# Transposing queries, keys and attention outputs by DMA instead of on TensorE from batch 2 on, with output stores issued from GpSimd's queue and loads one step earlier

## The chip, the cores and the metric

The kernel runs on one core of a Trainium2 chip. The metric is device time in microseconds (us). Engines: PE is TensorE (PEld its weight loads), DVE is VectorE, ACT is ScalarE, POOL is GpSimd, SP is SyncE. DMAs are issued from POOL's queue (software descriptors) and from SP's queue (hardware descriptors).

## The reference

Attention with a relative position bias for 8 batches of 8 heads, 576 positions, head size 64; its output is x, 4608 x 512, which goes through a bilinear feed-forward network (FFN) of width 1536:

```python
scores = q @ k.T / 8 + bias[bucket(i - j)]          # per batch and head, 576 x 576
attn_out = softmax(scores) @ v
x = attn_out.transpose(0, 2, 1, 3).reshape(4608, 512)
out = ((x @ w_a) * (x @ w_b)) @ w_out
```

## The kernel before

It works in steps. Step s computes scores and exponentials for head pair s (32 pairs, four to a batch) and the value products of pair s - 1. From step 4 on it mixes in "units" of the FFN, for a chunk of 512 tokens from an earlier batch: a group of four matmuls each, 36 units to a chunk, nine to a step (about 11.9 us). So a chunk lasts four steps. Its last twelve units are the four output tiles, three units each, and these fall mostly at the end of a step 4b - 1 and in step 4b. I call step 4b the boundary.

TensorE transposes queries, keys and attention outputs, since matmuls need the head dimension on the partitions:

```python
def transposes(ps, src, p, tag):
    b, hp = divmod(p, 4)
    for t in range(NM):                       # NM = 4
        x = (st[p][tag][:, t, :, :] if early(b) else
             src[b % 2][:, 512 * t + 128 * hp:512 * t + 128 * hp + 128])
        nc.tensor.transpose(ps[:, 128 * t:128 * t + 128], x, ident[:, :])
# t_q(p): four of these for queries, one for both tails, copies PSUM -> SBUF on DVE
# t_k(p): four for keys, copies on DVE
def t_x(p, eng=None):                         # attention outputs of pair p -> xn, the FFN's input
    ps = ps_tr.tile([128, 1024], BF16, tag="tr", name=f"trx{p}")
    for jq in range(5):
        nc.tensor.transpose(ps[:, 128 * jq:128 * jq + 128], XG[p % 2][:, jq, :, :], ident[:, :])
    copy(eng, xn_sb[hp][:, SM * b:SM * b + SM], ps[:, 0:SM])
    ...
```

An output tile is copied from PSUM by ACT into `ob`, which has two slots (`wrk` has `bufs=2`), and stored from SP's queue. The FFN's PSUM pool also has two buffers:

```python
ob = wrk.tile([128, DM], FP32, tag="ob", name=f"ob{c}_{tt}")
nc.scalar.activation(out=ob[:, :], in_=po[:, :], func=ACTF.Copy)
...
nc.sync.dma_start(out=out[r0:r0 + 128, :], in_=ob[:, :])
```

Loads go out from POOL, which runs its queue in order:

```python
b = s // 4 + 1
if s > 4 and s % 4 == 1 and b < B:
    load_q(b, 0, 8); load_k(b, 0, 8); load_tails(b); load_v(b, 0, 8); load_vt(b)
```

The softmax here doesn't subtract the row's maximum and nothing guards it: scores larger than these inputs give would overflow.

Of the kernel before, what the change touches and what calls it, by code (L numbers as in the profile page):

```python
# [13 lines left out]
def kernel(  # L14
# [11 lines left out]
    nc = tc.nc  # L26
    FP32 = mybir.dt.float32
    BF16 = mybir.dt.bfloat16
# [3 lines left out]
    B, H, S, Dh = 8, 8, 576, 64  # L32
    NB = 32
    NM = 4
    SM = 128 * NM
    ST = S - SM
# [4 lines left out]
    NDF = DF // 128  # L41
    NMC = DM // 128
    NP = B * H // 2
    scale = 1.0 / 8.0

    const = ctx.enter_context(tc.tile_pool(name="const", bufs=1))
    wpool = ctx.enter_context(tc.tile_pool(name="wpool", bufs=1))
# [41 lines left out]
    qn = [wpool.tile([128, H * NM * Dh], BF16, name=f"qn{i}") for i in range(2)]  # L89
    kn = [wpool.tile([128, H * NM * Dh], BF16, name=f"kn{i}") for i in range(2)]  # L90
    vn = [wpool.tile([128, H * NM * Dh], BF16, name=f"vn{i}") for i in range(2)]
    qkt = [wpool.tile([128, H, Dh], BF16, name=f"qkt{i}") for i in range(2)]
    vm = [wpool.tile([128, H, NM, Dh + 1], BF16, name=f"vm{i}") for i in range(2)]
    vt = [wpool.tile([128, H // 2, 2, Dh + 1], BF16, name=f"vt{i}") for i in range(2)]

    QT = [wpool.tile([128, S + 2 * ST], BF16, name=f"QT{i}") for i in range(3)]
    KT = [wpool.tile([128, SM + 2 * ST], BF16, name=f"KT{i}") for i in range(3)]
# [12 lines left out]
    def early(b):  # L110
        return b < 2
# [24 lines left out]
    def load_v(b, h0, h1):  # L136
        load4(v, vn[b % 2], b, h0, h1)

    def load_tails(b):
        for src, o in ((q, 0), (k, 64)):  # L140
            nc.gpsimd.dma_start(out=qkt[b % 2][o:o + 64, :, :],
                                in_=src[b, :, SM:S, :].transpose([1, 0, 2]))

    def load_vt(b):
        for hh in range(2):
            nc.gpsimd.dma_start(  # L146
                out=vt[b % 2][64 * hh:64 * hh + 64, :, hh, 0:Dh],
                in_=v[b, hh:H:2, SM:S, :].transpose([1, 0, 2]))
# [84 lines left out]
        nc.vector.memset(KT[i][64:128, SM:SM + ST], 0.0)  # L233


    st = [dict() for _ in range(NP)]

    def copy(eng, out, in_):
        if eng is nc.scalar:
# [23 lines left out]

    def t_q(p, eng=None):
        b, hp = divmod(p, 4)
        ps = ps_tr.tile([128, 1024], BF16, tag="tr", name=f"trq{p}")
        transposes(ps, qn, p, "qr")
        nc.tensor.transpose(ps[:, SM:SM + 128], qkt[b % 2][:, 2 * hp:2 * hp + 2, :], ident[:, :])  # L268
        qT, kT = QT[p % 3], KT[p % 3]
        if early(b):  # L270
            copy(eng, qT[:, 0:SM].rearrange("d (p t) -> d p t", t=NM),
                 ps[:, 0:SM].rearrange("d (t p) -> d p t", t=NM))
            copy(eng, qT[:, SM:S], ps[:, SM:S])
        else:
            copy(eng, qT[:, 0:S], ps[:, 0:S])
        for hh in range(2):
            r = slice(64 * hh, 64 * hh + 64)
            nc.vector.tensor_copy(out=kT[r, SM + ST * hh:SM + ST * hh + ST], in_=ps[r, S:S + ST])
            nc.vector.tensor_copy(out=qT[r, S + ST * hh:S + ST * hh + ST], in_=ps[r, SM:S])

    def t_k(p, eng=None, pool=None, tag="tr"):
        b, hp = divmod(p, 4)
        ps = (pool or ps_tr).tile([128, 1024], BF16, tag=tag, name=f"trk{p}")
        transposes(ps, kn, p, "kr")
        copy(eng, KT[p % 3][:, 0:SM], ps[:, 0:SM])
        st[p]["at"] = [None] * NM

    def v_in(b, h0, h1):
        if b < 2:
# [4 lines left out]


    def qk(p, t0):
        qT, kT = QT[p % 3], KT[p % 3]
        for t in (t0, t0 + 1):
            ps = ps_sc.tile([128, 2, 512], FP32, tag="sc", name=f"qk{p}_{t}")
            for hh in range(2):  # L300
                r = slice(64 * hh, 64 * hh + 64)
                nc.tensor.matmul(out=ps[:, hh, :], lhsT=kT[r, 128 * t:128 * t + 128],  # L302
                                 rhs=qT[r, 0:SM], start=True, stop=True)
            st[p]["ps", t] = ps

    def ex(p, t):
# [9 lines left out]


    def qk_tail(p):
        hp = p % 4
        qT, kT = QT[p % 3], KT[p % 3]  # L320
        ps = ps_sc.tile([128, 2, 512], FP32, tag="sc", name=f"qkt{p}")
        for t in range(NM):
            nc.tensor.matmul(
                out=ps[:, 0, :].rearrange("p (h t c) -> p h t c", h=2, t=NM)[:, :, t, :],
                lhsT=kT[:, 128 * t:128 * t + 128], rhs=qT[:, S:S + 2 * ST],
                start=True, stop=True)
        nc.tensor.matmul(out=ps[:, 1, :], lhsT=kT[:, SM:SM + 2 * ST], rhs=qT[:, 0:SM],
                         start=True, stop=True)
        pt = ps_tr.tile([128, 512], FP32, tag="tr", name=f"qktt{p}")
        nc.tensor.matmul(out=pt[:, 0:ST], lhsT=kT[:, SM:SM + 2 * ST], rhs=qT[:, SM:S],  # L330
                         start=True, stop=True)
        st[p]["ps"] = (ps, pt)

    def ex_tail(p):
# [55 lines left out]

    def t_x(p, eng=None):
        b, hp = divmod(p, 4)
        ps = ps_tr.tile([128, 1024], BF16, tag="tr", name=f"trx{p}")
        for jq in range(5):
            nc.tensor.transpose(ps[:, 128 * jq:128 * jq + 128], XG[p % 2][:, jq, :, :], ident[:, :])  # L395
        copy(eng, xn_sb[hp][:, SM * b:SM * b + SM], ps[:, 0:SM])
        copy(eng, xn_sb[hp][:, SM * B + ST * b:SM * B + ST * b + ST], ps[:, SM:S])
        st[p].clear()
# [22 lines left out]
    def ff_o(c, tt, part):  # L421
        if part == 0:
            ff["po"] = ps_ff.tile([128, 512], FP32, tag="ffn", name=f"po{c}_{tt}")
        po = ff["po"]
        for df in range(4 * part, 4 * part + 4):
            nc.tensor.matmul(out=po[:, :], lhsT=g_sb[df][:, 128 * tt:128 * tt + 128],  # L426
                             rhs=wo_sb[:, df, :], start=(df == 0), stop=(df == NDF - 1))
        if part == 2:
            ob = wrk.tile([128, DM], FP32, tag="ob", name=f"ob{c}_{tt}")
            nc.scalar.activation(out=ob[:, :], in_=po[:, :], func=ACTF.Copy)  # L430
            if c < B:
                r0 = S * c + 128 * tt
                nc.sync.dma_start(out=out[r0:r0 + 128, :], in_=ob[:, :])
            else:
                for hh in range(2):
                    r0 = S * (2 * tt + hh) + SM
                    nc.sync.dma_start(out=out[r0:r0 + ST, :], in_=ob[64 * hh:64 * hh + 64, :])

    units = []
    for c in range(NCH):  # L440
# [55 lines left out]
    for s in range(4, NP + 1):  # L496
        new = s < NP
        U = "unit"
        A = lambda *jq: (lambda: [av(s - 1, j) for j in jq])
        steps = []  # L500
        if new:
            steps += [lambda: (qk(s, 0), ex(s, 0))]
        if s == 4:
            steps += [A(0, 1, 2), lambda: ex(s, 1), lambda: t_q(s + 1), A(3, 4),
                      lambda: mul(s, 0), lambda: t_x(s - 1), U, lambda: mul(s, 1), U,
                      lambda: (qk(s, 2), ex(s, 2)), U, lambda: ex(s, 3), lambda: t_k(s + 1), U,
                      lambda: mul(s, 2), U, lambda: mul(s, 3), lambda: (qk_tail(s), ex_tail(s)),
                      U, U, lambda: mul_tail(s)]
        elif new:
            steps += [U, lambda: ex(s, 1), A(0, 1, 2), U, lambda: mul(s, 0)]  # L510
            if s + 1 < NP:
                steps += [lambda: t_q(s + 1)]
            steps += [U, lambda: mul(s, 1), lambda: (qk(s, 2), ex(s, 2)), U, lambda: ex(s, 3)]
            if s + 1 < NP:
                steps += [lambda: t_k(s + 1)]
            steps += [U, lambda: mul(s, 2), A(3, 4), U, lambda: mul(s, 3),
                      lambda: (qk_tail(s), ex_tail(s)), U, lambda: t_x(s - 1), U,
                      lambda: mul_tail(s), U]
        else:
            steps += [A(0, 1, 2), U, U, U, A(3, 4), U, U, U, lambda: t_x(s - 1), U, U, U]  # L520
        reorder(s + 1)
        b = s // 4 + 1
        if s > 4 and s % 4 == 1 and b < B:
            load_q(b, 0, 8)
            load_k(b, 0, 8)
            load_tails(b)
            load_v(b, 0, 8)
            load_vt(b)
        quota = quotas.get(s, 9)
        seen, put = 0, 0  # L530
        nu = sum(1 for x in steps if x is U)
        for x in steps:
            if x is U:
                seen += 1
                n = (quota * seen + nu - 1) // nu - put
                put_units(n)
                put += n
            else:
                x()
        if new:  # L540
            v_next(s)
# [31 lines left out]
```

## Time and profile before

| | before |
|---|---|
| time | 450.62 us (450.6 to 450.64, 2 runs) |
| PE busy | 424.7 us, 95% of the span |
| chain of waits that ended last | PE 83% |
| 85 to 350 us: PE busy, granted clock | 262.64 of 265 us, 1.00 |

The first lines are from the page: busy time and share of each engine; the chain by engine. The last is a line of the windows view: the stretch, its length, then busy us and instruction counts of PE, PEld, DVE, ACT and POOL, the granted clock, the DMA share and GB/s.

```profile
PE 424.7 (95%) x3578; PEld 221.1 (49%) x3643; DVE 287.4 (64%) x838; ACT 245.8 (55%) x350; POOL 88.9 (20%) x117
...
PE 83%; DVE 10%; DMA 3%; issue 2%; ACT 1%; SPq 0%; DVEq 0%; ACTq 0%
...
85.00:350.00 265.00, 262.64 (x2402) 140.53 (x2446) 188.22 (x547) 160.41 (x224) 43.29 (x54) 1.00 0.43 52
```

TensorE is the limit after the ragged start. What a transpose costs is read from the timeline (start, duration, engine, line, operation), at the starts of the matmuls around it: durations overlap, starts do not.

```profile
161.44 0.38 PE L406 MATMUL pa_6_2485<-xn_122,wa_114 128*128 128x512 bf16 x1
161.65 0.38 PE L406 MATMUL pa_6_2485<-xn_123,wa_114 128*128 128x512 bf16 x1
161.87 0.39 PE L262 MATMUL trk_2494<-ident,kn_96 128*128 128x128 bf16 x4
162.09 0.38 PE L416 MATMUL pb_6_2500<-xn_120,wb_117 128*128 128x512 bf16 x1
```

Two matmuls of a group are 0.215 us apart; with four transposes in between it is 0.44 us (161.65 to 162.09). So four cost 0.225 us, and five, read in the same way, 0.285 us.

The queues of SP and POOL at one boundary, from the timeline. The four stores of a chunk go out as soon as their tile is copied; four query loads (and four key loads) keep POOL busy 3.5 us.

```profile
180.48 0.33 SPq L433 DMA_DIRECT2D out_dram<-ob_0_2749  x1
184.94 0.33 SPq L433 DMA_DIRECT2D out_dram<-ob_1_2818  x1
189.08 0.33 SPq L433 DMA_DIRECT2D out_dram<-ob_2_2875  x1
192.42 0.33 SPq L433 DMA_DIRECT2D out_dram<-ob_3_2914  x1
...
207.26 3.53 POOL L123 DMA_DIRECT2D qn_93<-in_q_dram  x4 [18.47 <-PE trq_3162 L268]
210.76 3.54 POOL L132 DMA_DIRECT2D kn_95<-in_k_dram  x4
```

### The profile page before, as it was taken

The numbers are of one execution on the slowest core, as the hardware profiler recorded it, in microseconds if no ns is written. First come the engines' busy times: TensorE is split into PE (matmuls) and PEld (weight loads), VectorE is DVE, ScalarE is ACT, GpSimd is POOL, SyncE is SP. The second block draws the span as 40 slices with busy tenths as digits, with TensorE's granted clock in tenths as the row PEclk, the third lists the DMA queues.
The fourth block names the chain that finished last, engine by engine and source line by source line (L and its number), as shares of the span: only waits on it lengthen the run. The fifth ranks groups of instructions, "written<-read, shape, count | busy, mean of one in ns | idle before, by whom it ended". The sixth has DMA issues, their size and how long they took to land.

```text
span 449.3 us, 9012 instructions
## 1 busy us (share of the span) xinstructions
PE 424.7 (95%) x3578; PEld 221.1 (49%) x3643; DVE 287.4 (64%) x838; ACT 245.8 (55%) x350; POOL 88.9 (20%) x117
## 2 busy tenths in 40 slices
PE   5676999999999999999999999999999999999995
PEld 2264455555555555555555555555555554444442
DVE  5579789668766787577856786587658862330320
ACT  2678566556655665566556665566556652322321
POOL 9456365010801070105200350100000000000000
PEclk8579999999999999999999999999999999999999
DMA  9999999420942097207912290200010002002004
GB/s 101 219 200 203 192 148 76 82 65 1 107 72 63 15 84 72 77 25 49 104 49 54 16 137 27 76 1 1 23 71 2 1 1 94 1 0 93 1 1 94
DMA packets 87370, 30.35 MB, mean 68 GB/s; under 512 B 64760, under 2 KB 82712, under 8 KB 87328
## 3 DMA queue, kind: packets, MB, share of 16 engines
q0 software_dynamic: 80144, 18.88, 45.0%
q1 hardware_dynamic: 6992, 10.86, 7.3%
q8 instruction: 28, 0.46, 0.4%
q14 instruction: 14, 0.11, 0.1%
q10 hardware_dynamic: 192, 0.03, 0.0%
HBM read 39.18 MB, written 9.45 MB: 108 GB/s over the span
## 4 chain that ended last, share of the span: by engine, by line
PE 83%; DVE 10%; DMA 3%; issue 2%; ACT 1%; SPq 0%; DVEq 0%; ACTq 0%
DMA Wt<-bias_tab 2%; DVE XG_111 L387 1%; DVE g_125 L419 1%; DVE g_124 L419 1%; PE warm L208 1%; PE po_1_1335 L426 1%; PE po_0_1275 L426 1%; DMA bias_tab<-tab_sb 1%; PE po_1_2057 L426 1%; PE po_1_4869 L426 1%; PE po_1_3463 L426 1%; PE po_1_2760 L426 1%; PE po_1_4166 L426 1%; PE po_2_1403 L426 1%; PE po_3_6071 L426 1%
## 5 line engine op out<-in xcount | busy, mean ns | idle before, releaser
L416 PEld LDWEIGHTS <-wb_118 128*128 128x128 bf16 x144 | 12.4, 97 | 16.6 <-issue 5.6
L406 PEld LDWEIGHTS <-wa_114 128*128 128x128 bf16 x144 | 12.5, 98 | 15.3 <-issue 3.4
L416 PEld LDWEIGHTS <-wb_117 128*128 128x128 bf16 x144 | 12.4, 97 | 14.9 <-issue 4.7
L406 PEld LDWEIGHTS <-wa_113 128*128 128x128 bf16 x144 | 12.5, 98 | 14.6 <-issue 3.0
L416 PEld LDWEIGHTS <-wb_116 128*128 128x128 bf16 x144 | 12.3, 97 | 14.9 <-issue 5.1
L406 PEld LDWEIGHTS <-wa_115 128*128 128x128 bf16 x144 | 12.7, 98 | 13.4 <-issue 2.5
L123 POOL DMA_DIRECT2D qn_93<-in_q_dram x12 | 11.0, 925 | 38.6 <-PE trq_3162 L268 18.5
L123 POOL DMA_DIRECT2D qn_94<-in_q_dram x12 | 10.6, 886 | 40.2 <-PE trq_2459 L268 18.5
L146 POOL DMA_DIRECT2D vt_104<-in_v_dram x8 | 4.9, 620 | 53.7 <-PE av_3_2848 L376 17.3
L132 POOL DMA_DIRECT2D kn_95<-in_k_dram x12 | 10.6, 906 | 6.8 <-DVE qr_844 L251 6.6
L146 POOL DMA_DIRECT2D vt_103<-in_v_dram x8 | 5.0, 640 | 34.8 <-PE av_3_2145 L376 17.3
L132 POOL DMA_DIRECT2D kn_96<-in_k_dram x12 | 10.6, 912 | 0.0
L395 PEld LDWEIGHTS <-XG_112 128*128 128x128 bf16 x80 | 5.8, 98 | 5.4 <-DVE XG_112 L387 1.5
L395 PEld LDWEIGHTS <-XG_111 128*128 128x128 bf16 x80 | 5.8, 98 | 5.1 <-DVE XG_111 L387 1.8
L302 PEld LDWEIGHTS <-KT_108 64*128 64x128 bf16 x88 | 2.8, 95 | 10.7 <-issue 8.6
L419 DVE TENSOR_TENSOR g_124<-pb_0_5871,ha_0_5869 128x512 bf16<-128x512 f32 x1 | 0.7, 692 | 11.4 <-PE pb_0_5871 L416 11.4
L302 PEld LDWEIGHTS <-KT_109 64*128 64x128 bf16 x88 | 2.6, 95 | 10.4 <-issue 10.4
L426 PEld LDWEIGHTS <-g_124 128*128 128x128 bf16 x36 | 3.5, 97 | 7.0 <-issue 4.7
L302 PEld LDWEIGHTS <-KT_110 64*128 64x128 bf16 x80 | 2.4, 95 | 8.2 <-issue 8.1
L114 POOL DMA_DIRECT2D vn_98<-in_v_dram x5 | 4.2, 836 | 7.4 <-DVE vm_102 L291 6.8
L426 PEld LDWEIGHTS <-g_126 128*128 128x128 bf16 x36 | 3.5, 98 | 4.3
L426 PEld LDWEIGHTS <-g_134 128*128 128x128 bf16 x36 | 3.5, 98 | 4.3
(3194 smaller groups left out, 1643.6 us busy)
## 6 DMA issues: line engine op xcount, KB each, us to landing
qn_93<-in_q_dram POOLq DMA_DIRECT2D x16, 128.0 KB, 4.2
kn_95<-in_k_dram POOLq DMA_DIRECT2D x16, 128.0 KB, 5.1
qn_94<-in_q_dram POOLq DMA_DIRECT2D x16, 128.0 KB, 5.4
kn_96<-in_k_dram POOLq DMA_DIRECT2D x16, 128.0 KB, 4.9
wo<-in_moe_w_out_dram POOLq DMA_DIRECT2D x1, 1536.0 KB, 16.4
vn_97<-in_v_dram POOLq DMA_DIRECT2D x3, 512.0 KB, 7.1
vn_98<-in_v_dram POOLq DMA_DIRECT2D x3, 512.0 KB, 5.8
vn_97<-in_v_dram POOLq DMA_DIRECT2D x2, 256.0 KB, 10.7
```

Source lines behind the costliest of these rows:

```text
L114: nc.gpsimd.dma_start(out=dst[:, 256 * h0:256 * h1].rearrange("p (h x) -> p h x", x=256), in_=src[b, h0:h1, 0:SM, :].rearrange("h (p t) d ...
L123: nc.gpsimd.dma_start(out=qn[b % 2][:, :].rearrange("p (t h d) -> p t h d", h=H, t=NM)[:, t, h0:h1, :], in_=q[b, h0:h1, 128 * t:128 * t + ...
L132: nc.gpsimd.dma_start(out=kn[b % 2][:, :].rearrange("p (t h d) -> p t h d", h=H, t=NM)[:, t, h0:h1, :], in_=k[b, h0:h1, t:SM:NM, :].transp ...
L146: nc.gpsimd.dma_start(out=vt[b % 2][64 * hh:64 * hh + 64, :, hh, 0:Dh], in_=v[b, hh:H:2, SM:S, :].transpose([1, 0, 2]))
L208: nc.tensor.matmul(out=warm[:, :], lhsT=zero_sb[:, 0:128], rhs=zero_sb[:, :], start=True, stop=True)
L302: nc.tensor.matmul(out=ps[:, hh, :], lhsT=kT[r, 128 * t:128 * t + 128], rhs=qT[r, 0:SM], start=True, stop=True)
L387: nc.vector.tensor_tensor(out=xg[0:np_, j0:j0 + n, :, :], in0=pav[0:np_, s0:s0 + n, :, 0:Dh], in1=rc.unsqueeze(3).to_broadcast([np_, n, 2, ...
L395: nc.tensor.transpose(ps[:, 128 * jq:128 * jq + 128], XG[p % 2][:, jq, :, :], ident[:, :])
L406: nc.tensor.matmul(out=pa[:, :], lhsT=wa_sb[df // 4][:, mc, 128 * (df % 4):128 * (df % 4) + 128], rhs=xn_sb[mc][:, 512 * c:512 * c + 512], ...
L416: nc.tensor.matmul(out=pb[:, :], lhsT=wb_sb[df // 4][:, mc, 128 * (df % 4):128 * (df % 4) + 128], rhs=xn_sb[mc][:, 512 * c:512 * c + 512], ...
L419: nc.vector.tensor_tensor(out=g_sb[df][:, :], in0=pb[:, :], in1=ff["ha"][:, :], op=MULT)
L426: nc.tensor.matmul(out=po[:, :], lhsT=g_sb[df][:, 128 * tt:128 * tt + 128], rhs=wo_sb[:, df, :], start=(df == 0), stop=(df == NDF - 1))
```

## The change

Its intent is to take transposes off TensorE. From batch 2 on, four transposing DMAs a batch, issued from SP, turn queries, keys and their zero-padded tails; two a pair turn the attention outputs. Stores move from SP's queue to POOL's, so that SP's is free for transposes. The loads move one step earlier, to the boundary step, so that the transposes can follow in time.

```diff
+    def turn(b):
+        i = b % 2
+        for src, dst in ((qn, QTb), (kn, KTb)):
+            nc.sync.dma_start_transpose(
+                out=dst[i][:, :, :, :].rearrange("d t h p -> d (t h) p"), in_=src[i][:, :])
+        for src, dst in ((qtl, QTt), (ktl, KTt)):
+            nc.sync.dma_start_transpose(
+                out=dst[i][:, :, :], in_=src[i][:, :, :, :].rearrange("p h a d -> p (h a d)"))
 ... (t_q and t_k return at once for these batches; qk and qk_tail read QTb, KTb, QTt, KTt)
-        nc.tensor.matmul(out=pt[:, 0:ST], lhsT=kT[:, SM:SM + 2 * ST], rhs=qT[:, SM:S],
-                         start=True, stop=True)
+        for hh in range(2):
+            nc.tensor.matmul(out=pt[:, 0:ST], lhsT=kTt_(p), rhs=qTt_(p)[:, ST * hh:ST * hh + ST],
+                             start=(hh == 0), stop=(hh == 1))
 ... (t_x)
+        if p >= XD:                                        # XD = 8
+            nc.sync.dma_start_transpose(
+                out=xn_sb[hp][:, SM * b:SM * b + SM].rearrange("d (t p) -> d t p", t=NM),
+                in_=XG[p % 2][:, 0:4, :, :].rearrange("p j a d -> p (j a d)"))
+            ... (and the 64 tail rows)
+            return
 ... (ff_o)
-                nc.sync.dma_start(out=out[r0:r0 + 128, :], in_=ob[:, :])
+                nc.gpsimd.dma_start(out=out[r0:r0 + 128, :], in_=ob[:, :])
 ... (main loop)
-        if s > 4 and s % 4 == 1 and b < B:
+        if s % 4 == 0 and b < B and new:
             load_q(b, 0, 8)
             load_k(b, 0, 8)
             load_tails(b)
             load_v(b, 0, 8)
+        if s % 4 == 1 and b < B:
             load_vt(b)
+        if s % 4 == 3 and b < B:
+            turn(b)
```

More of the change, by code (lines that the diff above doesn't have):

```diff
@@ L43 @@
     NP = B * H // 2
+    XD = 8
     scale = 1.0 / 8.0
@@ L92 @@
     qkt = [wpool.tile([128, H, Dh], BF16, name=f"qkt{i}") for i in range(2)]
+    qtl = [wpool.tile([128, H // 2, 2, Dh], BF16, name=f"qtl{i}") for i in range(2)]
+    ktl = [wpool.tile([128, H // 2, 2, Dh], BF16, name=f"ktl{i}") for i in range(2)]
+    QTb = [wpool.tile([128, NM, H // 2, 128], BF16, name=f"QTb{i}") for i in range(2)]
+    KTb = [wpool.tile([128, NM, H // 2, 128], BF16, name=f"KTb{i}") for i in range(2)]
+    QTt = [wpool.tile([128, H // 2, 128], BF16, name=f"QTt{i}") for i in range(2)]
+    KTt = [wpool.tile([128, H // 2, 128], BF16, name=f"KTt{i}") for i in range(2)]
     vm = [wpool.tile([128, H, NM, Dh + 1], BF16, name=f"vm{i}") for i in range(2)]
@@ L139, in load_tails @@
     def load_tails(b):
+        if not early(b):
+            for src, dst in ((q, qtl), (k, ktl)):
+                for hh in range(2):
+                    nc.gpsimd.dma_start(
+                        out=dst[b % 2][64 * hh:64 * hh + 64, :, hh, :],
+                        in_=src[b, hh:H:2, SM:S, :].transpose([1, 0, 2]))
+            return
         for src, o in ((q, 0), (k, 64)):
@@ L233, with kT_, qT_, kTt_ @@
         nc.vector.memset(KT[i][64:128, SM:SM + ST], 0.0)
+    for i in range(2):
+        for x in (qtl, ktl):
+            nc.gpsimd.memset(x[i][0:64, :, 1, :], 0.0)
+            nc.gpsimd.memset(x[i][64:128, :, 0, :], 0.0)
     st = [dict() for _ in range(NP)]
+    def turn(b):
[6 more added lines that the diff above has]
+                out=dst[i][:, :, :], in_=src[i][:, :, :, :].rearrange("p h a d -> p (h a d)"))
+    def kT_(p, t):
+        b, hp = divmod(p, 4)
+        return KT[p % 3][:, 128 * t:128 * t + 128] if early(b) else KTb[b % 2][:, t, hp, :]
+    def qT_(p):
+        b, hp = divmod(p, 4)
+        return QT[p % 3][:, 0:SM].rearrange("d (t p) -> d t p", t=NM) if early(b) else QTb[b % 2][:, :, hp, :]
+    def kTt_(p):
+        b, hp = divmod(p, 4)
+        return KT[p % 3][:, SM:SM + 2 * ST] if early(b) else KTt[b % 2][:, hp, :]
+    def qTt_(p):
+        b, hp = divmod(p, 4)
+        return QT[p % 3][:, S:S + 2 * ST] if early(b) else QTt[b % 2][:, hp, :]
     def copy(eng, out, in_):
@@ L265, in t_q @@
         b, hp = divmod(p, 4)
+        if not early(b):
+            return
         ps = ps_tr.tile([128, 1024], BF16, tag="tr", name=f"trq{p}")
@@ L282, in t_k @@
         b, hp = divmod(p, 4)
+        st[p]["at"] = [None] * NM
+        if not early(b):
+            return
         ps = (pool or ps_tr).tile([128, 1024], BF16, tag=tag, name=f"trk{p}")
@@ L285, in t_k @@
         copy(eng, KT[p % 3][:, 0:SM], ps[:, 0:SM])
-        st[p]["at"] = [None] * NM
     def v_in(b, h0, h1):
@@ L296, in qk @@
     def qk(p, t0):
-        qT, kT = QT[p % 3], KT[p % 3]
+        qT = qT_(p)
         for t in (t0, t0 + 1):
@@ L301, in qk @@
                 r = slice(64 * hh, 64 * hh + 64)
-                nc.tensor.matmul(out=ps[:, hh, :], lhsT=kT[r, 128 * t:128 * t + 128],
-                                 rhs=qT[r, 0:SM], start=True, stop=True)
+                nc.tensor.matmul(out=ps[:, hh, :], lhsT=kT_(p, t)[r, :],
+                                 rhs=qT[r, :, :], start=True, stop=True)
             st[p]["ps", t] = ps
@@ L318, in qk_tail @@
     def qk_tail(p):
-        hp = p % 4
-        qT, kT = QT[p % 3], KT[p % 3]
         ps = ps_sc.tile([128, 2, 512], FP32, tag="sc", name=f"qkt{p}")
@@ L324, in qk_tail @@
                 out=ps[:, 0, :].rearrange("p (h t c) -> p h t c", h=2, t=NM)[:, :, t, :],
-                lhsT=kT[:, 128 * t:128 * t + 128], rhs=qT[:, S:S + 2 * ST],
+                lhsT=kT_(p, t), rhs=qTt_(p),
                 start=True, stop=True)
-        nc.tensor.matmul(out=ps[:, 1, :], lhsT=kT[:, SM:SM + 2 * ST], rhs=qT[:, 0:SM],
+        nc.tensor.matmul(out=ps[:, 1, :], lhsT=kTt_(p), rhs=qT_(p),
                          start=True, stop=True)
         pt = ps_tr.tile([128, 512], FP32, tag="tr", name=f"qktt{p}")
-        nc.tensor.matmul(out=pt[:, 0:ST], lhsT=kT[:, SM:SM + 2 * ST], rhs=qT[:, SM:S],
-                         start=True, stop=True)
+        for hh in range(2):
+            nc.tensor.matmul(out=pt[:, 0:ST], lhsT=kTt_(p), rhs=qTt_(p)[:, ST * hh:ST * hh + ST],
+                             start=(hh == 0), stop=(hh == 1))
         st[p]["ps"] = (ps, pt)
@@ L392, in t_x @@
         b, hp = divmod(p, 4)
+        if p >= XD:
+            nc.sync.dma_start_transpose(
+                out=xn_sb[hp][:, SM * b:SM * b + SM].rearrange("d (t p) -> d t p", t=NM),
+                in_=XG[p % 2][:, 0:4, :, :].rearrange("p j a d -> p (j a d)"))
+            o = SM * B + ST * b
+            nc.sync.dma_start_transpose(
+                out=xn_sb[hp][:, o:o + ST].unsqueeze(1),
+                in_=XG[p % 2][0:64, 4, :, :].rearrange("p a d -> p (a d)"))
+            st[p].clear()
+            return
         ps = ps_tr.tile([128, 1024], BF16, tag="tr", name=f"trx{p}")
@@ L436, in ff_o @@
                     r0 = S * (2 * tt + hh) + SM
-                    nc.sync.dma_start(out=out[r0:r0 + ST, :], in_=ob[64 * hh:64 * hh + 64, :])
+                    nc.gpsimd.dma_start(out=out[r0:r0 + ST, :], in_=ob[64 * hh:64 * hh + 64, :])
     units = []
```

## The prediction

> What bounds the kernel now. The windows view has TensorE busy 29.74 of every 30 us from 100 to 340 us, at granted clock 1.00, and the chain of waits is 83% PE. DVE (64%), ACT (55%) and POOL (20%) have room. After about 60 us time moves one for one with work taken from TensorE's stream, or a wait put into it.
>
> Removed. From pair 8 on, each pair loses 5 transposes for queries and their tail, 4 for keys and 5 for attention outputs. In the timeline, 4 key transposes push the next matmul group from the usual 0.215 us to 0.44 us after its predecessor (0.225 us net), a group of 5 to 0.50 us (0.285 us net). Per pair 0.285+0.225+0.285 = 0.795 us; 24 pairs: 19.1 us, all on the critical path. DVE's copies go too, worth nothing here. Added on TensorE: one 64-column matmul in each of 32 tails, estimated 0.04 us each, 1.3 us. Net about -18 us, 433 us, if everything else hides.
>
> What I expect not to hide:
> 1. Stores move behind loads. POOL's queue now has, in order, the first store of a chunk, the 13 loads of a batch, then stores two to four. In the trace four q loads take 3.53 us of POOL, four k loads 3.53, a 64-partition load 0.62, the v load 0.89: 10.5 us of issue. Today stores two to four follow the first by 4.4, 8.6 and 11.9 us, on SP's queue, and land in 2.0 us. Store two will be issued about 11.5 us after the first and lie behind the v load (5.8 to 7.1 us to landing), so it lands after 15 to 17.5 us. The output buffer has two slots: the fourth copy on ACT, due at about 11 us, waits for that store, 3 to 6 us. TensorE has about 1.8 us of work (scores and one FFN group) before it needs the same PSUM buffer. Estimate 1 to 4.5 us lost at each of 5 boundaries (steps 8, 12, 16, 20, 24): about 3 us each, 15 us. If TensorE idles long enough the clock can fall as well (the Trainium skill, "TensorE: Matmul & The Clock Gate", gives about 3.4 us of idle; this trace shows clock 0.50 only in its ragged start).
> 2. The last pair of a batch now reaches the FFN through a DMA. Today the PE transposes precede the chunk that reads them by about 3.5 us; a DMA takes 2 us or more to land. 0 to 1 us at each of 7 boundaries.
> 3. The last stores go by software descriptors: up to +1 us.
> The batch transposes (1.25 MB per batch) have a whole step, 11 us; the Trainium skill, "DMA: Bandwidth & Descriptors", latency table, gives 261 GB/s for transposing DMAs, an estimate of 5 us. No run here shows it yet. They should hide.
>
> Sum: 450.6 - 18 + 15 + 2 + 1, about 450. I predict 449 us, range 433 to 466; faster 0.28, same 0.45, slower 0.27.
>
> What would show it. Right: about 336 fewer transposes; steps of about 11.1 us where no batch load starts; gaps on TensorE and ACT at the start of the steps after 8, 12, 16, 20, 24, released by an output store; store two landing 15 us after store one. Wrong: if ACT never waits for store two, the time is near 434 us. If the batch transposes take over 11 us, TensorE waits for them at steps 8, 12, ... and the time goes beyond 466 us; likewise, at the first FFN group of each chunk, if a transposing DMA is much slower beside loads.

## The result, and the profile after

The changed kernel is correct and slower: 475.2 us (473.42 and 476.98, 2 runs) against 450.62. The ratio is 1.0551, 95% interval 1.0455 to 1.0646. A ratio here is the mean time of one kernel's fast runs over that of the other's of the same rounds, so it is not quite the ratio of the medians quoted.

The same lines of the changed kernel:

```profile
PE 420.8 (89%) x3280; PEld 206.3 (44%) x3339; DVE 248.8 (53%) x646; ACT 245.3 (52%) x350; POOL 119.9 (25%) x177
...
issue 41%; PE 32%; DMA 14%; POOL 11%; DVE 0%; ACT 0%; POOLq 0%; ACTq 0%; DVEq 0%
...
85.00:350.00 265.00, 236.95 (x1928) 115.60 (x1960) 139.42 (x336) 145.05 (x203) 68.27 (x94) 0.94 0.78 90
```

The trace has 298 matmuls fewer (336 transposes go and 32 tail matmuls come; a few records are missing). Yet PE's busy time fell by only 3.9 us, with a granted clock of 0.94 on average from 85 to 350 us; the same instructions with the clock at 1.00 there (e3 below) are busy for 409.4 us, 15.3 less than before. And in that stretch PE is now idle 28 us instead of 2.4. The chain of waits is no longer mostly PE's.

The view of waits (who waited for what; us in total, times, longest) names the places, for PE and then for ACT:

```profile
PE pb L473 <- ACT ob L487: 19.0, 5, 4.8
PE pa L463 <- DMA xn<-XG: 6.8, 4, 2.2
...
ACT ob L487 <- DMA out_dram<-ob: 43.1, 5, 9.6
```

Five times ACT waits some 8.6 us to copy an output tile, until an earlier store has freed its slot. Five times PE waits for that copy. Four times it waits for attention outputs that a DMA transposes. The numbers add up: 19.0 + 6.8 = 25.8 us, and PE's idle time rose by 28.05 - 2.36 = 25.7.

One boundary in the timeline, first the queue of POOL, then the last output transpose on SP's queue, then PE and ACT:

```profile
135.52 0.57 POOL L490 DMA_DIRECT2D out_dram<-ob  x1 [31.91 <-ACT ob L487]
136.08 3.54 POOL L130 DMA_DIRECT2D qn<-in_q_dram  x4
139.56 3.55 POOL L139 DMA_DIRECT2D kn<-in_k_dram  x4
143.02 1.34 POOL L150 DMA_DIRECT2D qtl<-in_q_dram  x2
144.24 1.34 POOL L150 DMA_DIRECT2D ktl<-in_k_dram  x2
145.45 1.03 POOL L121 DMA_DIRECT2D vn<-in_v_dram  x1
146.33 1.27 POOL L490 DMA_DIRECT2D out_dram<-ob  x2
153.99 0.55 POOL L490 DMA_DIRECT2D out_dram<-ob  x1 [6.38 <-ACT ob L487]
...
142.33 1.20 SPq L441 DMA_TRANSPOSE xn<-XG  x1
...
142.97 2.75 PE L483 MATMUL po<-wo,g 128*128 128x512 bf16 x11
149.03 0.38 PE L463 MATMUL pa<-xn,wa 128*128 128x512 bf16 x1 [2.01 <-DMA xn<-XG]
153.10 0.60 ACT L487 ACTIVATE ob<-po 128x512 f32<-128x512 f32 x1 [8.74 <-DMA out_dram<-ob]
153.75 1.86 PE L473 MATMUL pb<-xn,wb 128*128 128x512 bf16 x4 [2.96 <-ACT ob L487]
```

Read it from the top. Store one leaves at 135.5. Thirteen loads follow, 10.2 us of POOL's time. The copy of store two's tile had begun at 138.8 us, but the store leaves only at 146.3, behind all of them. The fourth tile is complete in PSUM at 145.7 (142.97 + 2.75). ACT copies it at 153.1, when store two's slot is free: 7.4 us late. Meanwhile the output transpose issued at 142.33 is there only at 149.03, 6.7 us later, where an undisturbed one takes 2.4 us. PE has two gaps, 2.0 us for that transpose and 3.0 us for the copy.

After the first gap the granted clock falls. This is the windows view, in four stretches of a quarter of a us; the clock is the third number from the end.

```profile
148.75:149.00 0.25, 0.00 (x0) 0.00 (x0) 0.00 (x0) 0.00 (x0) 0.00 (x0) 1.00 1.20 113
149.50:149.75 0.25, 0.25 (x11) 0.25 (x8) 0.00 (x0) 0.00 (x0) 0.00 (x0) 0.76 1.29 168
149.75:150.00 0.25, 0.25 (x9) 0.25 (x7) 0.00 (x0) 0.00 (x0) 0.00 (x0) 0.50 1.46 193
...
156.50:156.75 0.25, 0.25 (x2) 0.00 (x0) 0.25 (x1) 0.00 (x0) 0.00 (x0) 1.00 1.28 81
```

It is 0.50 from about 149.6 until about 156.4 (the stretches left out in between have 0.50 as well, up to the last one). So three things cost time at a boundary: the copy's wait, the late transpose, and a clock that is at half speed when work resumes.

### The profile page after: what moved, and what is told of

Its sections match the earlier page's. It is cut to its first block, busy times and chain, and to the rows that moved or that the text cites. A ratio compares the mean times of both kernels' runs of the same rounds, so it can differ in the third digit from the quotient of the medians.

```text
span 471.6 us, 8441 instructions
## 1 busy us (share of the span) xinstructions
PE 420.8 (89%) x3280; PEld 206.3 (44%) x3339; DVE 248.8 (53%) x646; ACT 245.3 (52%) x350; POOL 119.9 (25%) x177
## 4 chain that ended last, share of the span: by engine, by line
issue 41%; PE 32%; DMA 14%; POOL 11%; DVE 0%; ACT 0%; POOLq 0%; ACTq 0%; DVEq 0%
PE pb L473 10%; PE po L483 9%; PE pa L463 9%; DMA kn<-in_k_dram 4%; POOL qn L130 3%; DMA qn<-in_q_dram 3%; POOL kn L139 2%; DMA wa<-in_moe_w_a_dram 2%; DMA wb<-in_moe_w_b_dram 2%; PE av L423 2%; DMA vn<-in_v_dram 2%; PE qk L350 2%; DMA out_dram<-ob 1%; POOL out_dram L490 1%; POOL vt L160 1%
## 5 line engine op out<-in xcount | busy, mean ns | idle before, releaser
L357 ACT ACTIVATE at<-qk 128x1024 bf16<-128x1024 f32 x128 | 126.4, 1025 | 17.8 <-PE qk L350 17.8
L476 DVE TENSOR_TENSOR g<-pb,ha 128x512 bf16<-128x512 f32 x108 | 74.6, 691 | 111.3 <-PE pb L473 93.7
L473 PE MATMUL pb<-xn,wb 128*128 128x512 bf16 x410 | 113.2, 391 | 20.9 <-ACT ob L487 19.0
L463 PE MATMUL pa<-xn,wa 128*128 128x512 bf16 x421 | 114.7, 390 | 7.3 <-DMA xn<-XG 6.8
L467 ACT ACTIVATE ha<-pa 128x512 f32<-128x512 f32 x108 | 64.6, 598 | 76.5 <-PE pa L463 73.9
L483 PE MATMUL po<-wo,g 128*128 128x512 bf16 x410 | 99.4, 379 | 1.2
L362 DVE TENSOR_TENSOR at<-at,W 128x1024 bf16<-128x1024 bf16 x128 | 85.1, 683 | 9.3 <-ACT at L357 7.5
L463 PEld LDWEIGHTS <-wa 128*128 128x128 bf16 x432 | 39.9, 100 | 53.2 <-issue 16.2
L423 PE MATMUL av<-vm,at 128*128 128x65 bf16 x1024 | 49.9, 199 | 0.2 <-DVE at L362 0.2
L423 PEld LDWEIGHTS <-at 128*128 128x128 bf16 x1024 | 45.1, 101 | 6.6 <-DVE at L362 0.3
L414 PEld LDWEIGHTS <-att 128*128 128x128 bf16 x160 | 16.0, 100 | 17.1 <-issue 10.4
```

The lines of the kernel that those rows point to most:

```text
L357: nc.scalar.activation(out=at[:, :, :], in_=ps[:, :, :], func=ACTF.Exp, scale=scale)
L362: nc.vector.tensor_tensor(out=at[:, :, :], in0=at[:, :, :], in1=w[:, :, S - 1 + t:S - 1 + t - SM:-1], op=MULT)
L414: nc.tensor.matmul(out=pav[:, slot, :, :], lhsT=x, rhs=vt[i][:, hp, :, :], start=True, stop=True)
L423: nc.tensor.matmul(out=pav[:, slot, hh, :], lhsT=x, rhs=vm[i][:, 2 * hp + hh, t, :], start=False, stop=True, skip_group_check=True)
L463: nc.tensor.matmul(out=pa[:, :], lhsT=wa_sb[df // 4][:, mc, 128 * (df % 4):128 * (df % 4) + 128], rhs=xn_sb[mc][:, 512 * c:512 * c + 512], ...
L467: nc.scalar.activation(out=ha[:, :], in_=pa[:, :], func=ACTF.Copy)
```

## The experiments

Two theories stood at the start. Theory Q: the order of POOL's queue holds store two behind the loads, and the two output slots hand the delay to ACT and PE. Theory T: the transposing DMAs share the DMA engines with everything else and slow it, whichever queue the stores use. The kernel before took 450.2 to 450.9 us (medians). All results were correct.

| run | time, us | ratio to before | PE idle, 85 to 350 us | PE's wait for output copy | for attention outputs | for keys | clock, 85 to 350 us |
|---|---|---|---|---|---|---|---|
| changed kernel | 475.2 | 1.0551 | 28.1 | 19.0 | 6.8 | 0 | 0.94 |
| e1 stores on SP | 467.8 | 1.0378 | 23.7 | 0 | 9.0 | 13.2 | 0.96 |
| e2 four slots | 445.9 | 0.9905 | 9.9 | 0 | 7.7 | 0 | 0.99 |
| e3 loads later | 435.9 | 0.9682 | 2.2 | 0 | 0 | 0 | 1.00 |
| e4 outputs by PE | 490.9 | 1.0899 | 41.0 | 38.5 | 0 | 0 | 0.93 |
| e5 before, with the new queue order | 487.4 | 1.0847 | 25.1 | 22.3 | 0 | 0 | 0.96 |
| e7 gaps filled | 468.8 | 1.0397 | 9.4 | 3.5 | 1.2 | 0 | 1.00 |
| e10 stores on SP, loads held | 435.5 | 0.9662 | 2.2 | 0 | 0.4 | 0 | 1.00 |
| e12 v load later | 452.2 | 1.0043 | 14.0 | 3.0 | 7.1 | 0 | 1.00 |
| e11 loads later, outputs by PE | 441.5 | 0.9811 | 2.9 | 0 | 0 | 0 | 1.00 |
| e9 loads later, last stores on SP | 433.2 | 0.9618 | 2.2 | 0 | 0 | 0 | 1.00 |

The waits are of the whole span, and 85 to 350 us covers a different share of each kernel's work; both only serve to show what is there. A zero means that the view of waits lists none. One of e12's four runs (458.15 us) is slow; its time and ratio are from the other three (mean 452.28 us over 450.34). e8, a single run, is told in its section.

### e1: stores back on SP's queue

```diff
-                nc.gpsimd.dma_start(out=out[r0:r0 + 128, :], in_=ob[:, :])
+                nc.sync.dma_start(out=out[r0:r0 + 128, :], in_=ob[:, :])
```
(and the same for the last chunk)

> The changed kernel with one thing undone: output stores go out from SyncE's queue again; loads, DMA transposes all as in the change. Theory Q (POOL's queue holds store two behind 13 loads, two output slots make ACT and then TensorE wait): the 43 us of ACT waiting for an output store go to nearly 0, the 19 us of TensorE waiting for the output copy go to nearly 0, the four-step period of the disturbed chunks falls from about 52.7 us to about 46 to 47, and the time to 443 to 450 us. What stays is TensorE's wait for the last pair's transposed output beside the loads, about 2 us at each of 5 boundaries. Rival T (the transposing DMAs slow everything that shares the DMA engines, whichever queue the stores use): a store from SyncE still lands late, since it follows transposes and shares engines with loads, ACT still waits, and the time stays above 465 us.

Measured: 467.77 us. ACT no longer waits for a store at all, as theory Q has it, and stores land in 2.2 us (median). But the time lies in the range of rival T, above 465, though for another reason than the late store that T had named: a new wait took the place of the old one. Lines of the timeline, SP and POOL, and the wait on PE that ends them:

```profile
117.69 1.70 SPq L260 DMA_TRANSPOSE QTb<-qn  x1
119.37 0.90 POOL L121 DMA_DIRECT2D vn<-in_v_dram  x1 [16.59 <-DVE vm L339]
119.57 8.38 SPq L260 DMA_TRANSPOSE KTb<-kn  x1
...
133.06 0.60 PE L350 MATMUL qk<-QTb,KTb 64*128 64x512 bf16 x4 [3.99 <-DMA KTb<-kn]
```

With no store in POOL's queue, nothing holds the loads to the pace of the chunks. They run as far ahead as their buffers allow. The loads of later batches go out early, and the v load waits for its buffer and leaves exactly beside the batch's transposes. The transpose of keys is then issued over 8.4 us (3.6 us in the changed kernel) and takes 12.2 us to land instead of 5.7 (medians). So my expectation of 443 to 450 missed. Theory Q was right about the stores and silent about a second thing that the stores did in POOL's queue: they paced the loads. Theory T's mechanism, slowing beside loads, showed itself, though not on the stores.

### e2: four output slots

```diff
+    obp = ctx.enter_context(tc.tile_pool(name="obp", bufs=4))
-            ob = wrk.tile([128, DM], FP32, tag="ob", name=f"ob{c}_{tt}")
+            ob = obp.tile([128, DM], FP32, tag="ob", name=f"ob{c}_{tt}")
```

> The changed kernel with four output slots in place of two; stores still behind the loads on POOL's queue. Theory Q: store two still lands some 17 us after store one, but nobody waits for it within the chunk, so the ACT and TensorE waits vanish and the time is 443 to 450 us, as with the stores on SyncE. Rival T: the slots change little, above 465 us.

Measured: 445.91 us, in the range. Store two is still late, the waits for the slot are gone, and the late attention outputs are all that stays of PE's idle time: 9.86 - 2.16 = 7.7 us more than e3, and 7.7 us is that wait. This run shows that the two slots are the link between a late store and a stalled PE.

### e3: loads one step later, behind the chunk's stores

```diff
-        if s % 4 == 0 and b < B and new:
+        if s > 4 and s % 4 == 1 and b < B:
```

> The changed kernel with the batch's loads issued one step later (where the kernel before has them), after the chunk's four stores and after the last pair's transpose; stores still on POOL's queue. Theory Q with its second part (the last pair's transpose takes 6.7 us instead of 2.4 only because it runs beside the loads): both waits vanish, clock stays at 1.00 after 60 us, four-step period about 44.5 us throughout, time 431 to 437 us. Rival T: transposes beside loads still cost somewhere, time over 445 us. If the batch transposes now come too late for their step, TensorE waits for them at steps 8, 12, ... and the time is over 440.

Measured: 435.93 us, in the range; 0.9682 of the kernel before. The windows line and the chain of this run:

```profile
85.00:350.00 265.00, 262.84 (x2250) 131.30 (x2291) 163.67 (x396) 169.53 (x237) 71.05 (x98) 1.00 0.82 95
...
PE 87%; DVE 2%; issue 1%; ACT 0%; POOL 0%; POOLq 0%; DVEq 0%; ACTq 0%
```

One line of the program takes 39 us off the changed kernel (whose two runs lie 3.6 us apart, so the 39 is good to a few us). The loads now follow store four in POOL's queue and run when no output transpose is urgent: an output transpose beside them takes up to 7.7 us to land here too, but nobody waits for it. From store one to store one is 44.8 us (129.40, 174.22, 219.03 us), where the kernel before has 47.52 and the changed kernel 52.7 on average (135.52 to 346.30 us, four chunks). So the transposes on TensorE were worth 2.7 us a chunk, and the boundary costs 7.9 us.

### e4: attention outputs on PE again, the rest as changed

```diff
-    XD = 8
+    XD = NP
```

> The changed kernel with attention outputs transposed on TensorE again for all pairs; queries and keys still by DMA, stores still behind the loads. It adds 24 x 0.285 = 6.8 us of TensorE work. Theory Q: the end of each disturbed boundary is set by the landing of store two, 17.5 us after store one, so only the wait for the transposed output goes and the wait for the output copy grows by as much; time 470 to 481 us. Rival X (the late transposed output is what costs most): time 455 to 465 us.

Measured: 490.87 us, slower than either range. Removing the late output transposes gained nothing, but this run alone does not settle rival X, since it moved other transposes as well (below). e2 does: there the late outputs stay, PE waits 7.7 us for them, and the time is only 10 us above e3. Theory Q's number was too low here. The output transposes had been standing in SP's queue in front of the batch's, and so held them back. Without them the batch's transposes start as soon as the loads land, in the middle of the boundary:

```profile
147.83 3.85 SPq L260 DMA_TRANSPOSE QTb<-qn  x1
152.68 6.47 SPq L260 DMA_TRANSPOSE KTb<-kn  x1
```

There they meet the v load and store two (issued at 151.05). ACT's wait for a store grew from 43.1 to 54.9 us in total. The latest store took 10.4 us to land; in the changed kernel it was 7.6.

### e5: the kernel before, with only the new order of POOL's queue

```diff
-                nc.sync.dma_start(out=out[r0:r0 + 128, :], in_=ob[:, :])
+                nc.gpsimd.dma_start(out=out[r0:r0 + 128, :], in_=ob[:, :])
-        if s > 4 and s % 4 == 1 and b < B:
+        if s % 4 == 0 and b < B and new:
```
(`load_vt` stays at `s % 4 == 1`; the last chunk's stores move too)

> The kernel before, with only the change's queue order: stores issued from POOL, the batch's loads one step earlier, the late v tails where they were. No DMA transposes at all. Theory Q: store two again leaves POOL behind 12 loads, about 11 us after store one, lands behind the v load at about 16 us, and ACT's fourth copy, due at 11.9 us, waits some 4 us; TensorE loses 1 to 3 us at each of 5 boundaries; time 455 to 465 us. Rival T (only the transposes make the stores late): the time stays at 449 to 453 us.

Measured: 487.38 us. The waits of PE and ACT:

```profile
PE pb L416 <- ACT ob L430: 22.3, 5, 5.4
...
ACT ob L430 <- DMA out_dram<-ob: 38.6, 5, 8.8
```

There is no DMA transpose in this kernel (and 11 loads in front of store two, not the 12 that I had counted), and it loses 36.5 us (487.38 - 450.91). So theory T is not needed for the late stores; the queue order is enough. My number was too low here as in the prediction: ACT's wait was 38.6 us in five, 7.7 each, not 4, and I had again left out the clock (0.96).

### e7: the gaps filled with useless matmuls

```diff
+            late = s in (9, 13, 17, 21, 25)
+            steps += [lambda: fill(9)] if late else []     # 9 matmuls of zeros, 128x512
             steps += [U, lambda: ex(s, 1), A(0, 1, 2)]
+            steps += [lambda: fill(13)] if late else []
```

> The changed kernel with idle time of TensorE filled: at steps 9, 13, 17, 21, 25, 9 matmuls of zeros after the first scores and 13 after the first output products, 4.7 us of work at full clock in gaps of about 5 us. It adds work and takes no wait away. If the fall of the granted clock after the gaps is part of the loss: clock stays near 1.00 in these stretches and the time falls by 4 to 9 us, to 466 to 471. If it is not: 475 us or more.

Measured: 468.78 us, in the range: about 7 us faster by adding work ((1.0551 - 1.0397) x 450.6; the two intervals leave some 2 to 12 us). The windows line and ACT's wait:

```profile
85.00:350.00 265.00, 255.61 (x2082) 126.16 (x2123) 142.59 (x347) 148.09 (x208) 70.70 (x97) 1.00 0.79 92
...
ACT ob L487 <- DMA out_dram<-ob: 43.9, 5, 9.3
```

The clock stays at 1.00, and ACT's wait for stores is unchanged. So the fall of the clock is a cost of its own, about 7 of the 39 us, net of whatever the added matmuls cost.

### e8: stores on SP and the loads one step later in the program (one run)

The edits of e1 and e3 together.

> Stores from SyncE and the loads one step later in the program. POOL's queue then holds exactly the instructions of the run with stores on SyncE and loads early, in the same order. Theory R (with no store in POOL's queue nothing holds the loads back: they run steps ahead and meet the batch's transposes): as that run, 463 to 470 us, TensorE again waits for transposed keys. Rival (the place of the loads in the program decides): as the run with loads later and stores on POOL, 432 to 440 us.

Measured: 467.01 us in one run, as e1 and unlike e3; PE waits 12.5 us for keys. POOL's instructions are the same as in e1 and in the same order, and that decides. The place of the loads among the other engines' instructions in the program made less than 1 us of difference.

### e10: as e8, but the loads are held back

```diff
+            if "ob" in ff:       # the chunk's last output tile
+                nc.gpsimd.tensor_copy(out=gate_sb[0:1, 0:1], in_=ff["ob"][0:1, 0:1])
             load_q(b, 0, 8)
```
(and `ff["ob"] = ob` where the tile is copied)

> As the run before in this list, with one addition: before each batch's loads POOL copies one element of the chunk's last output tile, so the loads can't run ahead of the chunk's end. Stores stay on SyncE. Theory R: the loads no longer meet the transposes, the waits for transposed keys and outputs go, and the time is 431 to 438 us. Rival (stores and transposes in one queue of SyncE disturb each other): stays over 445 us.

Measured: 435.49 us. One element copied by POOL before each batch's loads takes 31.5 us off (467.01, a single run, minus 435.49). The rival, that stores and transposes in one queue of SP disturb each other, falls: they do not, to within what these runs resolve. Here it hardly matters which queue carries the stores (435.93 us in e3); when the loads run does.

### e12: only the v load later

```diff
             load_tails(b)
-            load_v(b, 0, 8)
         if s % 4 == 1 and b < B:
+            load_v(b, 0, 8)
             load_vt(b)
```

> The changed kernel with only the v load taken out from in front of the stores, to the next step; the 12 loads of queries, keys and tails stay in front. It splits the delay of store two: time to leave POOL's queue (about 10.6 us after store one instead of 11.4) and time behind the v load's data. If the v load's data is most of the lateness: store two lands 13.5 to 15 us after store one, ACT's wait falls from 8.6 to 2 to 4 us a boundary, TensorE's wait for the output copy to 0 to 1 us, and the transposed output of the last pair is still slow; time 444 to 455 us. If the order in POOL's queue alone is what counts: 468 to 474 us.

Measured: 452.15 us, the median of the three fast runs, in the range. At the boundary I looked at, store one left at 131.16, store two at 141.09, and the fourth copy began at 145.67: 14.5 us after store one, where it was 17.6 (153.10 - 135.52). ACT still waited 5.7 us, more than I expected, but PE's wait for the copy fell from 19.0 to 3.0 us. So of the 39 us, 23 (475.2 - 452.15) hung on the last, largest load in front of the stores; PE rode out most of the rest of ACT's wait.

### e11 and e9: what is left

e11 has the edits of e3 and e4; e9 has that of e3, and stores of the last two chunks from SP.

> Loads one step later, stores on POOL, and the attention outputs transposed on TensorE. It repeats the test of the transposed outputs where no load is in their way: 24 groups of five transposes at 0.285 us, so 6 to 7.5 us slower than the same kernel with outputs by DMA (435.9 us), 442 to 444 us. If the outputs by DMA cost TensorE hidden waits even there, the difference is smaller, under 4 us.

> Loads one step later, and the stores of the last two chunks, after the last loads and transposes, on SyncE's queue. Only the end differs: the last store is issued in two parts of about 0.5 us on POOL. If its way through POOL costs anything it is the last 1 us: 434 to 436 us.

Measured: 441.48 us for e11, 5.6 us slower than e3, just under the range of 442 to 444. So the attention outputs by DMA are worth nearly the 6.8 us of their transposes, once loads are out of their way. e9 ran in 433.17 us, just under its range of 434 to 436 and the best of all: 0.9618 of the kernel before, interval 0.9589 to 0.9646. In the profiles, the time from the end of the last output copy to the end is 3.9 us in e9 and 5.7 us in e3. That explains 1.8 us of the difference; the rest, 1 us, I leave open.

## Why the prediction was wrong

1. **What bounds the kernel, and the saving.** "After about 60 us time moves one for one with work taken from TensorE's stream": right. e3, with nothing in the way, has chunks 2.7 us shorter; the prediction's terms give 4 x (0.795 - 0.04) = 3.0 us. Over the whole run e3 saves 14.5 us and e9 17.0, of the 18 forecast.
2. **Step 1, the mechanism.** "POOL's queue now has, in order, the first store of a chunk, the 13 loads of a batch, then stores two to four": right in every link. e5 shows it without the transposes, e2 shows that the slots pass it on, e3 shows it gone.
3. **The size of a boundary: the step that failed.** The sum priced a boundary at "about 3 us each, 15 us" for the copy's wait and about 2 us in all for the last pair's outputs: 17 us, nearly all at five boundaries. A boundary costs 7.9 us, five cost 39. The copy's wait itself was not far off: PE waited 19.0 us for it, 2.4 to 4.8 us at a boundary, against "1 to 4.5". ACT's wait, "3 to 6" us, was 7.4 us from the moment the tile was complete (8.6 by the view of waits), because, at the boundary shown, store two landed at 17.6 us after store one rather than between 15 and 17.5, and the tile was complete after 10.2 us rather than 11. Most of the missing 22 us came from two things that the text named and the sum left out or set near zero, the clock (point 4) and the outputs' transpose beside the loads (point 5); some 6 us stay open.
4. **The clock, named and not counted.** "If TensorE idles long enough the clock can fall as well" stood in the text without a term in the sum. Its value, by e7, is about 7 us. The Trainium skill ("TensorE: Matmul & The Clock Gate", Part 1, "What's actually happening") gives an idle window of about 3.4 us, more than the 3 us of step 1. In the trace three of PE's five waits for the copy were longer than that (4.7, 4.8 and 4.1 us), and 2.0 us of idle was followed by a fall too.
5. **Step 2, the last pair's outputs.** "0 to 1 us at each of 7 boundaries" was right where no loads run at the boundary (e3: no wait). Beside loads the transpose takes 6.7 us instead of 2.4, and PE waited 6.8 us in four places. The prediction's last sentence named this ("if a transposing DMA is much slower beside loads") as a sign of being wrong, but the sum priced the transpose as if it ran alone, although step 1 puts the loads right beside it.
6. **Step 3, the end.** "Up to +1 us": e9 against e3 says 1.8 us.
7. **The batch transposes** do hide in the changed kernel. From the first issue at 123.2 us to the last landing it takes about 9.6 us (130.40 + 2.4 - 123.22), more than the estimated 5 and less than a step.

The loss of 39 us (475.2 - 435.9) is then: 25.8 us of PE's waits, about 7 us of clock, and some 6 us that I have not assigned. Since PE's waits and its clock act on each other, I would not divide it more finely.

## What to carry to other kernels

An in-order queue does two jobs: it carries transfers, and it paces whatever stands behind a wait in it. Before stores or loads are moved to another queue, write down for each queue what will stand in front of what, what each entry waits for, and how many slots there are between a late store and the engine that fills them. Then keep bulk loads away from the transposes that an engine is about to need: beside loads a short transpose took nearly three times as long, and the orders in which no urgent transpose met the loads (e3, e9, e10) were 14 to 17 us faster than the kernel before.

## What the Trainium skill lacked or had wrong

- "TensorE: Matmul & The Clock Gate" (Part 1, "What's actually happening") says that the clock falls after at least one idle window of about 3.4 us. Here shorter gaps were followed by a fall. In the changed kernel PE was idle from 147.0 to 149.0 us, and the clock went from 1.00 to 0.50 at about 149.6 us. In e2 a gap of 1.8 us (to 285.38 us) was followed by a fall at about 285.6 us. The length of a gap alone does not tell: two others in e2, of 2.1 and 2.2 us (to 191.43 and 238.62 us), left the clock at 1.00. In the changed kernel it came back after about 2.7 us of work (153.75 to 156.4).
- "DMA: Bandwidth & Descriptors" ("Issuing engines are not separate DMA queues") says that DMAs of all issuers run on the same 16 engines and interleave. These traces agree, and give what the page lacks, the price for a transpose beside loads: an output transpose took 2.4 us alone (median) and 6.7 us beside the loads (7.7 at most in e3); the transpose of keys took 5.7 us to land in the changed kernel and 12.2 in e1 (medians).
- The same page ("Rules for kernel authors") says that a transpose next to ordinary DMAs needs nothing. The line stands beside a warning of corrupted data, and for correctness it held in all runs. For time it did not: 6.7 us instead of 2.4.
- The same page's latency table gives 261 GB/s for transposing DMAs in one kernel (with a non-contiguous middle dimension). Here four SBUF to SBUF transposes, 1.31 MB, took about 9.6 us, or 137 GB/s with their fixed costs; 8.4 of the 9.6 us passed until SP had issued the last of them.
- No page that I used says that a store in an in-order queue also paces the loads behind it. Here that pacing was worth over 30 us (e8 against e10).
